# A planned instruction order made anew, and the last 64 rows of a weight prepared on 128 partitions

## The chip, the cores and the metric

The kernel runs on one core of one Trainium2 chip. The metric is the device time of one execution in microseconds (us); the times shown are medians of several runs. The core has five engines with an instruction queue each: TensorE (PE in the profile) multiplies matrices, VectorE (DVE), ScalarE (ACT) and GpSimd (POOL) work on elements, and SyncE (SP) issues most of the transfers. An engine takes its instructions strictly in the order in which they were written, and one that waits holds up all behind it on that engine.

## The reference, cut to what matters

```python
w = softmax(weight_gen, axis=-1)          # (8, 4224, 8 heads, 7 taps)
x_unf = 7 shifted copies of x             # x: (8, 4224, 192), zero-padded in front
y  = einsum('bshk,bskhg->bshg', w, x_unf) # a convolution with weights of its own at each token
xn = (y - mean(y)) / sqrt(var(y) + 1e-6) * g_ln
out = y + relu(xn @ w_ch1) @ w_ch2        # 192 -> 768 -> 192
```

## The kernel before, in words

**Tiling.** The 33,792 tokens lie on 128 partitions, 264 in a row on each. A "column" is one such token position, so one column is 128 tokens. The columns are worked off in parts (`PARTS`, L21: six of 4, six of 8, fifteen of 12, then 8 and 4), and within a part in chunks of 4 or 6 columns. The softmax has its own, larger pieces (`SOFT`, L22: 4, 8, then 12 at a time). The feed-forward part works on groups of 4 columns (512 tokens), 66 in all.

**The front half, per chunk.** SyncE loads x into a ring of 36 columns (L311) and the tap weights (L317). The softmax goes VectorE maximum (L340), GpSimd subtraction (L342), ScalarE exponential (L345), VectorE sum (L347) and so on; its result `wn` lies in PSUM. The convolution (`conv`, L370) is three products of two taps each into buffers called `pr` and one product of one tap into `y`, all on VectorE (L404). For taps 1 and 3, GpSimd issues a transfer that adds the second half of the `pr` buffer onto the first (L410, "add" below). GpSimd then adds four pieces onto `y` (L407): the two halves of tap pair 5 first, then the two results of the transfers. A chunk of 4 columns has 768 elements in each partition.

**The norm and the turn.** ScalarE takes sums (L448) and squares (L453) of `y`, one row of statistics follows on ScalarE and VectorE (L476 to L487), ScalarE scales (L499, `xh`) and writes a half-precision high part (L515, `hl`), GpSimd writes the low part (L517, also into `hl`), and SyncE issues a transposing transfer (L521, "turn") that makes `xT`, the layout that TensorE needs.

**The back half, per group.** TensorE multiplies `xT` with the first weight (L531). One group is three units; a unit is 16 wide matmuls, and eight narrow ones finish a unit and begin the next, so two units share them. A unit fills one of two `ph` buffers in PSUM. ScalarE evicts it with relu (L561, `hh`), VectorE evicts what half precision lost (L563, `hlo`), and then the `ph` buffer is free for the unit after the next. The second weight needs 4 outputs of 18 matmuls each per group (L600 to L602, `po`), VectorE adds them to `y` (L613), and SyncE stores `y` (L620).

**The weights.** They come as 64-bit words and are turned into 32-bit numbers by `from_double` (L652: one ScalarE square, four VectorE steps, one ScalarE square with a sum), scaled by a power of two (`w_scale`, L687) and split into a high and a low half-precision part (L741 to L761). The first weight has 192 rows: 128 of them lie on 128 partitions (`a`), and the last 64 on the first 64 partitions alone (`c`). Transfers (`shift`, L748) copy half-precision rows to the other 64 partitions, where the layout of `xT` wants them. The second weight (`c2`) is turned in three pieces, and its low part is made by GpSimd at L780.

**What sets the order.** Nothing is written straight away. Each step becomes an `Op` (L66) with an engine, an estimated cost and a due time `want`, which is the column where it is used less a lead from a table (`WANT`, L30, `W_WANT` for the weights, `FIRST` for a correction in the first 12 columns). `Plan.order` (L92) then plays the program through once: at each step it takes, for each engine, the ready step with the smallest due time among those that could start within `AHEAD` ns of the earliest, and places the earliest of these, provided that its due time is within `WINDOW` columns of the oldest unplaced step. The written order follows from the planned start times. Adds and turns are kept apart: a turn waits until the add planned before it has landed, and an add for the turn (L117, L153 to L156, L812).

Of the kernel before, what the change touches and what calls it, by code (L numbers as in the profile page):

```python
# [9 lines left out]
F32 = mybir.dt.float32  # L10
# [6 lines left out]
P = 128  # L17
# [31 lines left out]
class Op:  # L49
    __slots__ = ("rank", "eng", "cost", "want", "fn", "lat", "dma", "deps", "nxt", "left", "ready",  # L50
                 "bufs", "start", "end", "kind", "behind")


class Plan:


    DMA_START = {"SP": 900.0, "Pool": 650.0, "ACT": 1250.0}
# [8 lines left out]
    def op(self, eng, cost, want, fn, r=(), w=(), lat=120.0, dma=0.0, kind=None):  # L66
# [3 lines left out]
        o.rank, o.eng, o.cost, o.want, o.fn, o.lat, o.dma = len(self.ops), eng, cost, want, fn, lat, dma  # L70
# [21 lines left out]
    def order(self):  # L92
        tenant = {p: [None] * len(t) for p, t in self.pools.items()}
        free, cand, dma_free, out = {}, {}, 0.0, []

        last, clear = {"add": None, "turn": None}, {"add": 0.0, "turn": 0.0}
        for o in self.ops:
            o.left = len(o.deps)
            for d in o.deps:
                d.nxt.append(o)  # L100
            cand.setdefault(o.eng, [])
            free[o.eng] = 0.0
            if not o.left:
                cand[o.eng].append(o)
# [21 lines left out]

        by_want, lead = sorted(self.ops, key=lambda o: o.want), 0
        while len(out) < len(self.ops):
# [24 lines left out]
            if o.kind:  # L153
# [14 lines left out]
def kernel(  # L168
# [72 lines left out]
    def dma_ns(n):  # L241
        return n * P / 370.0
# [45 lines left out]
    def sp(want, fn, r, w, dma, kind=None):  # L288
        op("SP", 1400 if kind else 450, want, fn, r=r, w=w, dma=dma, kind=kind)

    def load_x(ch):
        t0, n = ch["S"], ch["n"]
        want = t0 - WANT["load"]
        if t0 == 0:

            def first():
# [5 lines left out]
            sp(want, first, [], [("x", "h"), *cols], dma_ns((PAD + n) * D))  # L302
            src = bass.AP(tensor=xf.tensor, offset=0, ap=[[PB * C * D, B], [1, n * D]])
            sp(want, lambda: SY.dma_start(X[0:B, PAD : PAD + n, :].rearrange("p t d -> p (t d)"), src), [],
               [("x", "f")], 300.0)
            return
        if t0 % RING == 0:
            op("ACT", 1050, t0 - WANT["conv"] - 3,
# [3 lines left out]
           [xkey(t) for t in range(t0, t0 + n)], dma_ns(n * D * 4))  # L312

    def load_w(pa):
        t0, n = pa["S"], pa["n"]
        wb = pa["w"] = Buf("w")
        sp(t0 - WANT["wload"], lambda: SY.dma_start(at(wb)[:, :n, :].rearrange("p t f -> p (t f)"), tokens(wf, t0, n)), [], [wb],  # L317
           dma_ns(n * HK * 4))

    def early(s, what):  # L320
        return s - FIRST[what] * max(0.0, 1 - s / 12)

    def softmax(pa):
        n, S0, wb = pa["n"], early(pa["S"], "soft"), pa["w"]
# [11 lines left out]
        def step(eng, cost, name, fn, r, w):  # L336
            op(eng, cost, S0 - WANT[name], fn, r, w)
# [23 lines left out]
        step("V", 2 * v_ns(m, 20), "inv", newton, ["sm", rr], ["sm"])  # L361
# [482 lines left out]
```

## Time and profile before

| | us |
|---|---|
| median of 3 runs | 907.81 (907.77 to 909.34) |
| the profiled execution, as timed | 908.86 |
| its span in the profile | 907.1 |
| TensorE busy | 815.0 |
| VectorE busy | 785.3 |
| GpSimd busy | 696.6 |
| ScalarE busy | 676.5 |

The granted clock of TensorE was 0.992 of the full one over the span. The profile's views give times from the span's start. In a row of the timeline the first number is the start, the second the duration, then come engine, line, operation, output and input; in brackets stands how long the engine had been idle before and what released it. A row with x2 merges two instructions. Idle time of an engine that nobody waits for costs nothing.

### The profile page before, as it was taken

The numbers are of one execution on the slowest core, as the hardware profiler recorded it, in microseconds if no ns is written. First come the engines' busy times: TensorE is split into PE (matmuls) and PEld (weight loads), VectorE is DVE, ScalarE is ACT, GpSimd is POOL, SyncE is SP. The second block draws the span as 40 slices with busy tenths as digits, with TensorE's granted clock in tenths as the row PEclk, the third lists the DMA queues.
The fourth block names the chain that finished last, engine by engine and source line by source line (L and its number), as shares of the span: only waits on it lengthen the run. The fifth ranks groups of instructions, "written<-read, shape, count | busy, mean of one in ns | idle before, by whom it ended". The sixth has DMA issues, their size and how long they took to land. (4 is left out here: it accounts for less than half of the span.)

```text
span 907.1 us, 21485 instructions
## 1 busy us (share of the span) xinstructions
PE 815.0 (90%) x8716; PEld 729.6 (80%) x8716; DVE 785.3 (87%) x833; ACT 676.5 (75%) x1773; POOL 696.6 (77%) x403
## 2 busy tenths in 40 slices
PE   0035999999999999999999999999999999999997
PEld 0023898789888989898888898888988898799997
DVE  6897999999998989899798899988989979884342
ACT  2577878888878976986876896888698688599321
POOL 2799999998988788889877879878886986894000
PEclk9996999999999999999999999999999999999999
DMA  8867787798888777779776879867787666656111
GB/s 218 218 139 157 150 189 159 163 192 190 174 167 186 181 160 173 153 163 198 158 172 150 181 173 177 170 152 173 172 180 156 141 132 149 129 114 107 47 52 54
DMA packets 137996, 142.23 MB, mean 157 GB/s; under 512 B 107496, under 2 KB 108904, under 8 KB 137896
## 3 DMA queue, kind: packets, MB, share of 16 engines
q1 hardware_dynamic: 122983, 88.95, 42.3%
q0 software_dynamic: 14688, 51.91, 30.0%
q8 instruction: 68, 1.11, 0.5%
q14 instruction: 33, 0.26, 0.1%
q10 hardware_dynamic: 224, 0.00, 0.0%
HBM read 36.43 MB, written 25.95 MB: 69 GB/s over the span
## 5 line engine op out<-in xcount | busy, mean ns | idle before, releaser
L407 POOL TENSOR_TENSOR y<-y,pr 128x1152 f32<-128x1152 f32 (+1 forms) x204 | 506.0, 2516 | 71.4 <-DVE pr L404 66.4
L600 PE MATMUL po<-c_w2h,hh 128*128 128x192 f16 x1584 | 390.4, 246 | 0.0
L602 PE MATMUL po<-c_w2h,hlo 128*128 128x192 f16 x1584 | 390.0, 246 | 0.0
L601 PE MATMUL po<-c_w2l,hh 128*128 128x192 f16 x1584 | 390.0, 246 | 0.0
L531 PE MATMUL ph<-xT,c_w1h 128*128 128x256 f16 x2376 | 328.8, 275 | 26.0 <-DVE hlo L563 19.3
L404 DVE TENSOR_TENSOR pr<-x,wn 128x2304 f32<-128x2304 f32 (+1 forms) x153 | 337.3, 2216 | 9.7 <-POOL y L407 3.6
L563 DVE SCALAR_TENSOR_TENSOR hlo<-ph,hh 128x1024 f16<-128x1024 f32 x198 | 238.2, 1217 | 72.1 <-ACT hh L561 71.9
L531 PEld LDWEIGHTS <-c_w1h 128*128 128x128 f16 x2376 | 227.3, 99 | 69.9 <-issue 45.0
L561 ACT ACTIVATE hh<-ph 128x1024 f16<-128x1024 f32 x198 | 200.2, 1012 | 89.4 <-PE ph L531 86.6
L531 PE MATMUL ph<-xT,c_w1l 128*128 128x256 f16 (+1 forms) x1584 | 210.2, 274 | 7.3 <-DMA xT<-hl 5.8
L600 PEld LDWEIGHTS <-hh 128*128 128x128 f16 x1584 | 155.1, 98 | 7.6 <-issue 6.3
L601 PEld LDWEIGHTS <-hh 128*128 128x128 f16 x1584 | 155.2, 98 | 1.4 <-issue 0.2
L602 PEld LDWEIGHTS <-hlo 128*128 128x128 f16 x1584 | 155.1, 98 | 0.2 <-DVE hlo L563 0.2
L499 ACT ACTIVATE xh<-y,s 128x192 f32<-128x192 f32 x264 | 123.7, 535 | 31.8 <-DVE s L487 29.3
L531 PEld LDWEIGHTS <-c_w1l 128*128 128x128 f16 (+1 forms) x1584 | 108.8, 97 | 39.3 <-issue 21.3
L517 POOL TENSOR_TENSOR hl<-xh,hl 128x768 f16<-128x768 f32 x66 | 117.1, 1809 | 26.2 <-ACT hl L515 24.3
L410 POOL DMA_DIRECT2D pr<-pr x102 | 100.6, 1043 | 33.9 <-DVE pr L404 25.4
L453 ACT ACTIVATE junk<-y,s 128x192 f32<-128x192 f32 x264 | 119.4, 452 | 6.7
L448 ACT ACTIVATE junk<-y 128x192 f32<-128x192 f32 x264 | 95.1, 360 | 25.8 <-POOL y L407 20.0
L613 DVE SCALAR_TENSOR_TENSOR y<-po,c_fs,y 128x384 f32<-128x384 f32 x132 | 77.6, 608 | 17.3 <-PE po L602 17.3
L404 DVE TENSOR_TENSOR y<-x,wn 128x1152 f32<-128x1152 f32 (+1 forms) x51 | 60.0, 1179 | 0.0
L515 ACT ACTIVATE hl<-xh 128x768 f16<-128x768 f32 x66 | 55.0, 833 | 0.3
(62 smaller groups left out, 328.2 us busy)
## 6 DMA issues: line engine op xcount, KB each, us to landing
pr<-pr POOLq DMA_DIRECT2D x60, 576.0 KB, 6.1
x<-in_x_dram SPq DMA_DIRECT2D x30, 576.0 KB, 5.4
out_dram<-y SPq DMA_DIRECT2D x30, 576.0 KB, 4.5
pr<-pr POOLq DMA_DIRECT2D x42, 384.0 KB, 6.5
out_dram<-y SPq DMA_DIRECT2D x21, 384.0 KB, 4.0
x<-in_x_dram SPq DMA_DIRECT2D x20, 384.0 KB, 7.2
w<-in_weight_gen_dram SPq DMA_DIRECT2D x21, 336.0 KB, 6.1
pr<-in_moe_w_ch_dram SPq DMA_DIRECT2D x1, 1152.0 KB, 16.9
```

The lines of the kernel that those rows point to most:

```text
L404: V.tensor_tensor(out=ov, in0=xv, in1=wv, op=ALU.mult)
L407: E.tensor_tensor(out=flat(0), in0=flat(0), in1=flat(k), op=ALU.add)
L410: return Q.dma_start(flat(to), flat(k), accum_op=ALU.add, max_dma_last_dim=CHUNK * D * 4)
L453: A.activation(junk, at(y)[:, j, :], AF.Square, bias=at(s4)[:, 3, t : t + 1], accum_out=at(s4)[:, 0, t : t + 1])
L499: A.activation(at(xh)[:, t, :], at(y)[:, i, :], AF.Identity, bias=at(s4)[:, 3, g + t : g + t + 1], scale=at(s4)[:, 1, g + t : g + t + 1])
L517: lambda xh=xh, hl=hl: Q.tensor_tensor(out=halves(hl, True), in0=pairs(xh), in1=halves(hl, False), op=ALU.subtract),
L531: T_.matmul(at(gp["ph"][u])[:, r, v * 2 * P : (v + 1) * 2 * P], W[w][rows, wb, (2 * u + v) * P : (2 * u + v + 1) * P], xv[rows, r, xb, :, ...
L561: lambda: A.activation(at(hh)[:, us, :], at(ph), AF.Relu), [ph], [(hh, u)])
L563: lambda: V.scalar_tensor_tensor(out=at(hlo)[:, us, :], in0=at(ph), scalar=0.0, in1=at(hh)[:, us, :], op0=ALU.max, op1=ALU.subtract),
L600: T_.matmul(o, tok(hh, j), w2h[:, j, :], start=(j == 0), stop=False)
L601: T_.matmul(o, tok(hh, j), w2l[:, j, :], start=False, stop=False)
L602: T_.matmul(o, tok(hlo, j), w2h[:, j, :], start=False, stop=(j == NF - 1))
```

## The change

The diff leaves the computation and its tiling (`PARTS`, `SOFT`, all buffers) as they are, and changes four things.

1. **The table of leads.** `WANT` has two numbers for each kind of step: a lead, and what is added to it at column 0, falling to nothing at column 3.7 (`RAMP`). `W_WANT` and `FIRST` go; the weights' steps have entries in the same table, and more kinds have one of their own. `AHEAD` is 0. A step's due time is lowered to that of the earliest step that needs it.
2. **The planner's costs.** Each queue of transfers has its own free time in place of one for all, with 250 bytes per ns in place of 370; an issue costs 620 ns, in place of 450; a matmul block has a latency of 420, 80 or 360 ns, other steps 140.
3. **Loads.** They carry the kind "load" and are held to a window of their own (`NEAR`, 29.84 columns).
4. **The weight's last 64 rows.** Each row of 768 numbers is loaded as two halves on two partitions, so `from_double("c", ...)` and the scaling work on 128 partitions x 384. The high and low halves are made in a spare part of the tile `hh`, and eight transfers of 64 partitions x 384 put them in place, where before two of 64 x 768 did; the gain `g` of these rows is loaded twice.

```diff
-WANT = {'load': 38.96, 'wload': 44.01, 'max': 25.94, 'sub': 29.98, 'exp': 32.11, 'sum': 24.37,
...
-AHEAD = 55.78
-WINDOW = 20.72
+WANT = {'load': (-3.03, -19.38), 'wload': (75.89, -46.46), 'max': (34.08, -74.96), 'sub':
...
+RAMP = 3.7
+AHEAD = 0.0
+WINDOW = 20.41
+NEAR = 29.84
...
+        lead, more = WANT[want[0]]
+        s = want[1]
+        o.want = s - lead - more * max(0.0, 1 - s / RAMP)
...
+        for o in reversed(self.ops):
+            for d in o.deps:
+                d.want = min(d.want, o.want)
...
-            until = by_want[lead].want + WINDOW
+            until, near = by_want[lead].want + WINDOW, by_want[lead].want + NEAR
...
-                rows = [(t, o) for t, o in ((earliest(o), o) for o in c if o.want <= until)
+                rows = [(t, o) for t, o in ((earliest(o), o) for o in c
+                                          if o.want <= (near if o.kind == "load" else until))
...
-                dma_free = max(t + o.cost + self.DMA_START[o.eng], dma_free) + o.dma
-                o.end = dma_free + self.DMA_END
-            if o.kind:
+
+                begin = max(t + o.cost + self.DMA_START[o.kind if o.kind == "turn" else o.eng],
+                            dma_free.get(o.eng, 0.0))
+                dma_free[o.eng] = begin + o.dma * (1.0 if o.kind == "turn" else 1.2)
+                o.end = dma_free[o.eng] + self.DMA_END
+            if o.kind in clear:
...
-        dma("SP", SY, "load", lambda: words(1, 0, 2 * F)[top, :], w1b[P:D, :], 4 * F, raw[1])
+        dma("SP", SY, "load", lambda: words(1, 0, F),
+            bass.AP(tensor=w1b.tensor, offset=P * 2 * F, ap=[[F, 2], [2 * F, 64], [1, F]]), 4 * F, raw[1])
...
-        from_double("c", lambda: words(1, 0, 2 * F)[top], lambda: f32(wc, F)[top], F, s1[top, 1:2],
-                    [raw[1]], [wc], rows=top)
+        from_double("c", lambda: words(1, 0, F), lambda: f32(wc, F2), F2, s1[:, 1:2], [raw[1]], [wc])
...
+        def halves(w, tmp, r, name):
+            for i, rows in enumerate((top, bot)):
+                fs = slice(i * F2, (i + 1) * F2)
+                shift(w[top, 1, fs], lambda rows=rows: tmp()[rows], r, [(name + "1t", i)], F2)
+                shift(w[bot, 2, fs], lambda rows=rows: tmp()[rows], r, [(name + "2b", i)], F2)
```

Three places show how the order moves. The names in the rows: `pr` are product buffers, `y_67` to `y_71` the chunks 0 to 4, `hl_83` and `hl_84` the half-precision parts of groups 0 and 1, `xT_85` and `xT_86` what the turns of these groups write, `hh_88` and `hh_89` the raw rows of the first weight, `ph_103` and `ph_104` scratch for it. Lines above 310 are shifted by 15 to 30 in the changed kernel.

VectorE before, behind the first three products of chunk 0 and a sum of the softmax: the weight's steps, and at the end the third product of two taps of chunk 0, into `pr_78`.

```order
L672 TENSOR_SCALAR ph_103<-hh_89 64x768
L672 TENSOR_SCALAR ph_104<-hh_88 128x768
L675 SCALAR_TENSOR_TENSOR ph_103<-hh_89,ph_103 64x768
L675 SCALAR_TENSOR_TENSOR ph_104<-hh_88,ph_104 128x768
L678 SCALAR_TENSOR_TENSOR ph_103<-hh_89,ph_103 64x768
L678 SCALAR_TENSOR_TENSOR ph_104<-hh_88,ph_104 128x768
L357 SCALAR_TENSOR_TENSOR wn_102<-wn_102,rr_95 128x64
L358 SCALAR_TENSOR_TENSOR wn_102<-wn_102,rr_95 128x64
L682 SCALAR_TENSOR_TENSOR hlo_90<-pr_78,ph_104 128x768
L682 SCALAR_TENSOR_TENSOR hlo_90<-pr_79,ph_103 64x768
L340 TENSOR_REDUCE mx_92<-w_66 128x96
L404 TENSOR_TENSOR pr_78<-x,wn_102 128x2x768
```

VectorE now, from the first product of chunk 0 on:

```order
L423 TENSOR_TENSOR pr_76<-x,wn_102 128x2x768
L423 TENSOR_TENSOR pr_77<-x,wn_102 128x2x768
L361 TENSOR_REDUCE mx_93<-w_65 128x64
L423 TENSOR_TENSOR y_67<-x,wn_102 128x768
L423 TENSOR_TENSOR pr_79<-x,wn_102 128x2x768
L368 TENSOR_REDUCE wn_102<-e_97 128x64
L689 TENSOR_SCALAR ph_103<-hh_88 128x768
L361 TENSOR_REDUCE mx_92<-w_66 128x96
L692 SCALAR_TENSOR_TENSOR ph_103<-hh_88,ph_103 128x768
L689 TENSOR_SCALAR ph_104<-hh_89 128x384
```

The third product of chunk 0 (now into `pr_79`) moved ahead of all steps of the weight, behind one maximum and the product into `y_67`; the weight's rows with 64 partitions x 768 are rows with 384 elements now.

GpSimd before, from the low part of group 0 on to some rows behind that of group 1 (DMA rows are adds):

```order
L517 TENSOR_TENSOR hl_83<-xh_81,hl_83 128x2x384
L407 TENSOR_TENSOR y_69<-y_69,pr_80 128x768
L407 TENSOR_TENSOR y_69<-y_69,pr_78 128x768
L407 TENSOR_TENSOR y_69<-y_69,pr_79 128x768
L410 DMA pr_77<-pr_77 128x768
L410 DMA pr_76<-pr_76 128x768
L407 TENSOR_TENSOR y_70<-y_70,pr_80 128x768
L517 TENSOR_TENSOR hl_84<-xh_82,hl_84 128x2x384
L410 DMA pr_78<-pr_78 128x768
L407 TENSOR_TENSOR y_70<-y_70,pr_80 128x768
L410 DMA pr_79<-pr_79 128x768
```

GpSimd now, from the last row of chunk 1 on to the same place:

```order
L426 TENSOR_TENSOR y_68<-y_68,pr_76 128x768
L429 DMA pr_77<-pr_77 128x768
L429 DMA pr_80<-pr_80 128x768
L426 TENSOR_TENSOR y_69<-y_69,pr_78 128x768 x2
L429 DMA pr_76<-pr_76 128x768
L426 TENSOR_TENSOR y_69<-y_69,pr_77 128x768
L429 DMA pr_78<-pr_78 128x768
L426 TENSOR_TENSOR y_69<-y_69,pr_80 128x768
L532 TENSOR_TENSOR hl_84<-xh_82,hl_84 128x2x384
L426 TENSOR_TENSOR y_70<-y_70,pr_79 128x768 x2
L426 TENSOR_TENSOR y_70<-y_70,pr_76 128x768
```

Before, the low part of group 1 (`hl_84`) stood between the pieces of chunk 3 and had two adds close behind it; now it stands behind the last piece of chunk 2, its nearest add is two rows ahead of it, and the next one comes only behind three further pieces.

SyncE before, from the loads ahead of the weight's shifts to the turn of group 1:

```order
L311 DMA x<-in_x_dram 128x1x768 x3
L642 DMA pr_80<-in_moe_w_ch_dram 128x6x384
L317 DMA w_65<-in_weight_gen_dram 128x1x672
L311 DMA x<-in_x_dram 128x1x768
L748 DMA c_w1h<-c_w1h 64x768 x3
L748 DMA c_w1l<-c_w1l 64x768 x3
L317 DMA w_66<-in_weight_gen_dram 128x1x672
L311 DMA x<-in_x_dram 128x1x768
L521 DMA_TRANSPOSE xT_85<-hl_83 128x12x128
L311 DMA x<-in_x_dram 128x1x768 x2
L521 DMA_TRANSPOSE xT_86<-hl_84 128x12x128
```

SyncE now:

```order
L341 DMA w_66<-in_weight_gen_dram 128x1x672
L341 DMA w_64<-in_weight_gen_dram 128x1x672
L770 DMA c_w1h<-c_w1h 64x768 x2
L770 DMA c_w1h<-hh_89 64x384 x4
L770 DMA c_w1l<-c_w1l 64x768 x2
L770 DMA c_w1l<-hh_89 64x384 x4
L536 DMA_TRANSPOSE xT_85<-hl_83 128x12x128
L335 DMA x<-in_x_dram 128x1x768 x3
L536 DMA_TRANSPOSE xT_86<-hl_84 128x12x128
```

Six shifts (L748) became twelve (L770), and one load of x stands among these rows and the first turn no more; seven chunks of x are issued ahead of the first turn now, ten before.

More of the change, by code (lines that the diff above doesn't have):

```diff
@@ L50 @@
     __slots__ = ("rank", "eng", "cost", "want", "fn", "lat", "dma", "deps", "nxt", "left", "ready",
-                 "bufs", "start", "end", "kind", "behind")
+                 "bufs", "start", "end", "kind", "behind", "key")
 class Plan:
-    DMA_START = {"SP": 900.0, "Pool": 650.0, "ACT": 1250.0}
+    DMA_START = {"SP": 900.0, "Pool": 900.0, "ACT": 1250.0, "turn": -950.0}
     DMA_END = 1000.0
@@ L311, in load_x @@
         sp(want, lambda: SY.dma_start(X[:, xcol(t0) : xcol(t0) + n, :].rearrange("p t d -> p (t d)"), tokens(x, t0, n)), [],
-           [xkey(t) for t in range(t0, t0 + n)], dma_ns(n * D * 4))
+           [xkey(t) for t in range(t0, t0 + n)], dma_ns(n * D * 4), "load")
     def load_w(pa):
@@ L316, in load_w @@
         wb = pa["w"] = Buf("w")
[L317 to L321, printed above, removed]
+        sp(("wload", t0), lambda: SY.dma_start(at(wb)[:, :n, :].rearrange("p t f -> p (t f)"), tokens(wf, t0, n)), [], [wb],
+           dma_ns(n * HK * 4), "load")
     def softmax(pa):
-        n, S0, wb = pa["n"], early(pa["S"], "soft"), pa["w"]
+        n, S0, wb = pa["n"], pa["S"], pa["w"]
         m = n * H
@@ L547, in narrow_products @@
                        stop=(first and v == 1))
[L549 removed]
+    W1S = ["h0", "l0", "h1b", "l1b", "l2t", "h2t"] + [(k, i) for k in ("h1t", "l1t", "h2b", "l2b") for i in range(2)]
     def at_unit(unit):
@@ L559, in evict @@
         su = at_unit(unit)
-        op("ACT", a_ns(2 * NT * P, 50), su - WANT["relu"],
+        op("ACT", a_ns(2 * NT * P, 50), ("relu", su),
            lambda: A.activation(at(hh)[:, us, :], at(ph), AF.Relu), [ph], [(hh, u)])
-        op("V", v_ns(2 * NT * P, 6), su - WANT["hlo"],
+        op("V", v_ns(2 * NT * P, 6), ("hlo", su),
            lambda: V.scalar_tensor_tensor(
@@ L602, in mm @@
                 T_.matmul(o, tok(hlo, j), w2h[:, j, :], start=False, stop=(j == NF - 1))
-        op("PE", 1494, s, mm, [*((hh, u) for u in range(3)), *((hlo, u) for u in range(3)), "w2"],
-           [(po, h)])
+        op("PE", 1490, (f"o{t}", s), mm, [*((hh, u) for u in range(3)), *((hlo, u) for u in range(3)), "w2"],
+           [(po, h)], lat=360.0)
         if h == 0:
@@ L666, in tv @@
             return a[rows].bitcast(dt)[:, :n]
-        want = -W_WANT[want]
-        op("ACT", a_ns(n), want, lambda: A.activation(mv(), part(1).bitcast(F32), AF.Square), r, [m])
+        squared, want, normed = ((f"w_{want}{p}", 0) for p in "svn")
+        op("ACT", a_ns(n), squared, lambda: A.activation(mv(), part(1).bitcast(F32), AF.Square), r, [m])
         op("V", v_ns(n), want,
@@ L763, in weights @@
+        shift(w1l[bot, 1, :], lambda: w1l[top, 0, :], ["l0"], ["l1b"])
+        shift(w1l[top, 2, :], lambda: w1l[bot, 0, :], ["l0"], ["l2t"])
+        copy("w_h", lambda: f32(wc, F2), lambda: f32(wc, F2), F2, ["gi"], [wc], gi[:, 1:2])
+        low(lc, lambda: f32(wc, F2), hc, F2, [wc, (raw[1], "h")], [(raw[1], "l")])
+        halves(w1l, lc, [(raw[1], "l")], "l")
         tn = NF // 3 * D
```

149 lines of the change are left out of this document (74 added, 75 removed), and 3 rows, old and new, of the table WANT.

## The prediction

> **What bounds the kernel now.** I read the page first, then TensorE's waits, then the windows, then the timeline of the first 95 us.
>
> ```profile
> span 907.1 us, 21485 instructions
> PE 815.0 (90%) x8716; PEld 729.6 (80%) x8716; DVE 785.3 (87%) x833; ACT 676.5 (75%) x1773; POOL 696.6 (77%) x403
> ```
>
> TensorE is busy for 815.0 of 907.1 us, so 92.1 us are idle. Its waits say where they lie, over the span and (last row, asked for the window from 120 us on) in the long stretch:
>
> ```profile
> PE po L692 <- DVE c_s L732: 28.1, 1, 28.1
> PE po L692 <- DVE c_s L768: 25.5, 1, 25.5
> PE ph L531 <- DVE hlo L563: 20.8, 18, 2.6
> PE ph L531 <- DMA xT<-hl: 11.9, 2, 6.2
> ...
> PE ph L531 <- DVE hlo L563: 14.6, 15, 1.8
> ```
>
> The two waits at L692 are the start, before there is anything to multiply. What follows them is 11.9 us for two turns, and 20.8 us for `hlo`, the eviction that frees a `ph` buffer. 14.6 us of the latter, 15 waits with a mean of 0.97 us, lie behind 120 us; no other wait of TensorE is there. How fast TensorE can go when nobody holds it up stands in the chain of waits near the end, and what follows its last matmul too:
>
> ```profile
> 822.99 4.14 PE ph L531 x40
> ...
> 871.60 4.14 PE ph L531 x40
> ...
> 901.89 0.62 DVE y L613
> ```
>
> The pattern stands twice between these two rows, so it takes (871.60 - 822.99) / 2 = 24.3 us; it holds 120 matmuls at L531, six units with their narrow ones, that is two groups: 12.15 us a group, 802 us for all 66. So the span is a start, 802 us, what TensorE loses on the way, and a last eviction and store (907.1 - 901.9 = 5.2 us). The first matmuls show the start and the first loss (TensorE's timeline):
>
> ```profile
> 60.91 1.44 PE L531 MATMUL ph<-xT,c_w1h 128*128 128x256 f16 x6 [6.20 <-DMA xT<-hl]
> ...
> 77.96 0.61 PE L531 MATMUL ph<-xT,c_w1l 64*128 64x256 f16 x4 [5.75 <-DMA xT<-hl]
> 78.50 1.46 PE L531 MATMUL ph<-xT,c_w1h 128*128 128x256 f16 x6
> ...
> 90.98 0.83 PE L531 MATMUL ph<-xT,c_w1h 128*128 128x256 f16 x6
> ```
>
> 60.9 + 802 + 5.2 is 868.1, so 39.0 us of the span are lost on the way: 14.6 behind 120 us, and most of the rest ahead of 100 us, where TensorE waits for the second turn and runs at half pace (six products take 1.46 us at 78.5, 0.83 at 90.98). The windows agree:
>
> ```profile
> 60.00:80.00 20.00, 10.84 (x72) 7.06 (x72) 17.66 (x26) 17.54 (x46) 18.82 (x14) 0.90 0.73 159
> 80.00:100.00 20.00, 17.37 (x150) 14.18 (x149) 16.06 (x20) 14.46 (x42) 18.18 (x13) 0.76 0.62 127
> ...
> 700.00:800.00 100.00, 97.16 (x1048) 87.53 (x1047) 92.43 (x88) 76.47 (x208) 82.80 (x46) 1.00 0.64 134
> ```
>
> Columns: TensorE, weight loads, VectorE, ScalarE, GpSimd, then clock, DMA share, GB/s. In the ramp VectorE and GpSimd are nearly full and TensorE starves; later TensorE is full, VectorE close behind.
>
> **The change, part by part.** What counts is when the second group's `xT` lands, for until then TensorE has only three units to do in either kernel. The rows ahead of it, from four engines' timelines:
>
> ```profile
> 10.55 3.42 DVE L404 TENSOR_TENSOR pr<-x,wn 128x1536 f32<-128x1536 f32 x2 [3.48 <-DMA x<-in_x_dram]
> ...
> 24.17 1.74 DVE L404 TENSOR_TENSOR pr<-x,wn 128x1536 f32<-128x1536 f32 x1
> ```
> ```profile
> 25.99 3.71 POOL L407 TENSOR_TENSOR y<-y,pr 128x768 f32<-128x768 f32 x2 [0.24 <-DVE pr L404]
> ...
> 31.51 3.99 POOL L407 TENSOR_TENSOR y<-y,pr 128x768 f32<-128x768 f32 x2
> ...
> 55.87 1.63 POOL L517 TENSOR_TENSOR hl<-xh,hl 128x768 f16<-128x768 f32 x1
> ...
> 65.92 2.27 POOL L517 TENSOR_TENSOR hl<-xh,hl 128x768 f16<-128x768 f32 x1
> ...
> 69.86 1.84 POOL L410 DMA_DIRECT2D pr<-pr  x1
> ```
> ```profile
> 36.51 1.76 ACT L742 ACTIVATE c_w1h<-hlo,c_gi 128x768 f16<-128x768 f32 x2 [1.20 <-DVE c_gi L737]
> ...
> 50.49 0.83 ACT L515 ACTIVATE hl<-xh 128x768 f16<-128x768 f32 x1
> ```
> ```profile
> 57.53 1.54 SPq L521 DMA_TRANSPOSE xT<-hl  x1
> ...
> 74.72 1.40 SPq L521 DMA_TRANSPOSE xT<-hl  x1
> ```
>
> and the prices, from the groups kept apart by form (0 to 60 us) and the DMA issues of the same window (the second add row: 60 to 120 us):
>
> ```profile
> L404 DVE TENSOR_TENSOR pr<-x,wn 128x1536 f32<-128x1536 f32 x11 | 19.1, 1747 | 3.5 <-DMA x<-in_x_dram 3.5
> ...
> L672 DVE TENSOR_SCALAR po<-pr 128x384 int32<-128x384 int32 x3 | 1.6, 554 | 2.2 <-DMA pr<-in_moe_w_ch_dram 2.2
> ...
> L672 DVE TENSOR_SCALAR ph<-hh 64x768 int32<-64x768 int32 x1 | 1.0, 953 | 0.5 <-DMA hh<-in_moe_w_ch_dram 0.5
> ```
> ```profile
> L407 POOL TENSOR_TENSOR y<-y,pr 128x768 f32<-128x768 f32 x11 | 21.3, 1940 | 1.3 <-DVE c_s L768 0.8 <-DVE pr L404 0.2
> ...
> L410 POOL DMA_DIRECT2D pr<-pr x6 | 5.6, 941 | 11.5 <-DVE pr L404 11.5
> ...
> L745 POOL TENSOR_TENSOR c_w1l<-hlo,c_w1h 128x768 f16<-128x768 f32 x1 | 1.9, 1940 | 0.0
> ```
> ```profile
> pr<-pr POOLq DMA_DIRECT2D x6, 384.0 KB, 7.0
> ...
> c_w1h<-c_w1h SPq DMA_DIRECT2D x3, 96.0 KB, 2.1
> ```
> ```profile
> pr<-pr POOLq DMA_DIRECT2D x10, 384.0 KB, 4.6
> ```
>
> *Chunk 0 first.* Before, chunk 0's third product stood behind the weight's steps and began at 24.17, so its `y` was complete at 31.51 + 3.99 = 35.5. Now it follows the product into `y`: two products end at 10.55 + 3.42 = 14.0, then a maximum (0.5, in proportion to its 448 elements), half a product (0.9) and the third (1.75), 17.2 (x is also issued one place earlier, which I count at nothing). GpSimd adds two pieces (3.7) to 20.9, one subtraction of 672 elements (1.7 in proportion), and two more pieces (4.0): `y` is complete at 26.6, 8.9 us earlier.
>
> *The weight on 128 partitions.* 64 partitions cost as much as 128 (953 ns for 64 x 768), 384 elements 554: four VectorE steps save 0.4 us each, 1.6; two of ScalarE's copies and GpSimd's low part (1.94 to about 1.0) save as much in proportion. Six more shifts go onto SyncE's queue ahead of the first turn. Three issues in a row take 1.80 us at 37.47 in SyncE's timeline:
>
> ```profile
> 37.47 1.80 SPq L748 DMA_DIRECT2D c_w1h<-c_w1h  x3
> ```
>
> so four cost 2.4 us behind the low part's second half. The cover is GpSimd, which between that half and the low part of group 0 still has one addition (1.94) and the low part itself (1.63): 3.6 us. Cover gone, it would cost up to 2.4. [...]
>
> *The first turn.* GpSimd sets it. On VectorE, from 17.2: the weight's eight steps (4 x 0.95 + 4 x 0.55 = 6.0), some 5 us of softmax and scaling (2,900 elements at the product's rate, and a dozen small ones), three products and a half (6.1): chunk 1's third product ends near 34.5. GpSimd follows: addition 1.94, low parts 1.94 and 1.0, addition 1.94, low part of group 0 1.63: 43.0. ScalarE has the same work as between 36.5 and 51.3 before it (14.8 us, from 26.6 on: 41.4) and is no later. So the turn is issued at 43, not 57.53: 14.5 us earlier, and TensorE starts at 46.4.
>
> *The second turn.* Before, group 1's low part was done at 65.92 + 2.27 = 68.2, but the turn left at 74.72: it was kept apart from the add issued behind the low part, at 69.86. Now the nearest add stands ahead. From 43.0: two additions (3.9), three issues to the second add (0.9 each by its row, 2.7), two (3.9), one, the add of `pr_78`, one, the low part (1.94 + 0.9 + 1.94 + 1.63 = 6.4): 59.9. The add is issued 4.5 us ahead of that, at 55.4 to 56.3, and lands 4.6 to 7.0 us later, at 60 to 63.3. VectorE's third product for it is the eleventh pair: 11 x 1.75, and the rest of the queue, near 55. So the turn leaves at 60 to 64 in place of 74.72, 11 to 14.7 us earlier; 2 less if VectorE's product slips, 2 more if products and additions overlap as tightly as the two products in 3.42 us do. I take 13.5, bounds 9 and 17. Behind this turn SyncE holds loads of x; ten chunks are issued by then, and VectorE is at the fourth, so nobody waits for those.
>
> *The half pace.* TensorE started twice at half pace, at 60.9 and 77.96, and will start twice so again. The Trainium skill ("TensorE: Matmul & The Clock Gate", HAM oscillation) has it that an idle gap above 3.4 us halves the clock until about as long a stretch of work. By it the longer gap now (three units at half pace end near 54; a turn takes 3.4 us to the first matmul, 57.53 to 60.91, so the second ends it near 66) costs no more than before, and the sum stays.
>
> *Behind the ramp.* The tables and costs move hundreds of rows, and no row of the trace prices the new mix. What TensorE must cover is relu and `hlo`:
>
> ```profile
> L563 DVE SCALAR_TENSOR_TENSOR hlo<-ph,hh 128x1024 f16<-128x1024 f32 x198 | 238.2, 1217 | 72.1 <-ACT hh L561 71.9
> ...
> L561 ACT ACTIVATE hh<-ph 128x1024 f16<-128x1024 f32 x198 | 200.2, 1012 | 89.4 <-PE ph L531 86.6
> ```
>
> 2.2 us plus whatever stands ahead of them on their engines. Counted in TensorE's written order, a `ph` buffer finds one output or none between its last use and its next one 47 times of 196 before and 35 times now, three outputs or more 47 times before and 69 now. Bounds: all 14.6 us of `hlo` waits go, or they double. I take a little under half gone, 6.5, since VectorE's long products still stand in the queue ahead of `hlo`. Loads held back cost nothing unless x is late: a load is issued still some 18 columns ahead of the additions, over 50 us at 12.15 us per 4 columns, against landings of about 7.
>
> *Sum.* 908.86 (the profiled execution; 907.1 of span and 1.8 around it) - 13.5 - 6.5 = 888.9; it is 1.05 above the median of the runs, so 887.8, say 888.
>
> **The rivals.**
>
> *The early start is given back (901).* The ramp is bounded by GpSimd and VectorE (18.8 and 17.7 of 20 us busy), so groups may come so slowly that TensorE works in bursts. Each burst starts cold: the window from 80 to 100 lost 17.4 x 0.24 = 4.2 us by its clock of 0.76. Three such restarts in groups 2 to 6 return 12.6 of the 13.5. For it: both engines are full. Against: the front half had run ahead by 120 us without a further wait for a turn. 901 with the later gain.
>
> *VectorE's queue (slower, 928).* `hlo` stands in one queue with the products, and a new mix may put a product right ahead of it more often. Should one in four of the 198 units wait 0.97 us, 48.5 us replace 14.6: 907.8 - 13.5 + 33.9 = 928. It decides from 31 waits on, where gain and loss meet. Against: only 15 of some 185 units waited so far.
>
> *No waits at all (880).* Every `hlo` wait behind the ramp goes: 907.8 - 13.5 - 14.6 = 879.7. For it: TensorE's order has longer covers. Against: VectorE is 92% busy there.
>
> *The order is no better than the old one on the chip (907).* The planner's model differs from the chip, and gains and losses cancel.
>
> **How the numbers follow.** Forecast 0.62 (880 to 896), given back 0.15, no waits 0.11, VectorE's queue 0.08, no better 0.04. The range 876 to 903 holds the forecast, most of the no-waits case and nearly all of the given-back case. Faster by over 0.2% (1.8 us, about what a measurement can tell) is 0.62 + 0.15 + 0.11 = 0.88, the same 0.04, slower 0.08.
>
> **What would show it.** Right: first matmul at L546 near 46, the second turn's idle ending at 63 to 68, and TensorE's `hlo` waits behind 120 us near 8 us. Wrong: a second turn behind 70, several waits for xT behind 80 us, `hlo` waits above 20 us, or VectorE waiting for x.

## The result and the profile after

The changed kernel takes 903.21 us (median of 4 runs, 901.05 to 903.7), the kernel before 908.01 (4 runs): a ratio of 0.994 with a 95% interval of 0.9921 to 0.9959. It is faster by 4.8 us, where 20 were forecast. The profiled executions, 908.86 and 901.05 us, are 7.8 us apart: that of before lies above its median, that of after is the fastest of its four. So the profiles say where time went, and the medians how much. The other three runs of the changed kernel took 902.94 to 903.7 us at a granted clock of 0.985 to 0.986, against 901.05 at 0.991 in the profiled one; what they lost beyond it stands in no trace.

The page of the changed kernel, its first lines:

```profile
span 899.2 us, 21468 instructions
...
PE 813.2 (90%) x8716; PEld 728.8 (81%) x8716; DVE 781.7 (87%) x833; ACT 675.7 (75%) x1773; POOL 694.4 (77%) x403
```

TensorE's waits of the changed kernel, over the span and then from 120 us on (columns: us in total, times, longest):

```profile
PE po L709 <- DVE c_s L749: 33.7, 1, 33.7
PE ph L546 <- DMA xT<-hl: 27.6, 5, 18.8
PE ph L546 <- DVE hlo L578: 16.2, 17, 3.1
...
PE ph L546 <- DVE hlo L578: 13.0, 15, 3.1
PE ph L546 <- DMA xT<-hl: 2.9, 3, 1.6
```

Before, TensorE waited 14.6 us behind 120 us, all for `hlo`. Now it is 13.0 + 2.9 = 15.9. The forecast 6.5 us of gain there is not there at all. The ramp in TensorE's timeline:

```profile
53.02 1.44 PE L546 MATMUL ph<-xT,c_w1h 128*128 128x256 f16 x6 [18.76 <-DMA xT<-hl]
...
70.01 0.61 PE L546 MATMUL ph<-xT,c_w1l 64*128 64x256 f16 x4 [6.03 <-DMA xT<-hl]
```

The first matmul came at 53.0 (60.9 before, 46.4 forecast), and the second turn's wait ended at 70.0 (78.0 before, 63 to 68 forecast). So the second group came 7.95 us earlier, and the span gained as much: 907.1 - 899.2 = 7.9. The start is later than forecast for a reason that one row of VectorE shows, in the middle of the weight's steps. Here are two rows of the changed kernel, then the first step on the same rows of the weight before:

```profile
18.68 0.95 DVE L692 SCALAR_TENSOR_TENSOR ph<-hh,ph 128x768 int32<-128x768 int32 x1
26.75 0.56 DVE L689 TENSOR_SCALAR ph<-hh 128x384 int32<-128x384 int32 x1 [7.12 <-DMA hh<-in_moe_w_ch_dram]
```
```profile
16.11 1.81 DVE L672 TENSOR_SCALAR ph<-hh 64x768 int32<-64x768 int32 x2 [0.54 <-DMA hh<-in_moe_w_ch_dram]
```

In brackets: VectorE was idle for 7.12 us, until the load of the weight's last 64 rows had landed. Before, it had waited 0.54 us there. In the queue of SyncE both loads of the first weight were issued when they were before (4.30 there). The load of the second weight then stood in this queue until the rows had come (it was issued at 17.44 before). The rows below are SyncE's issues, its wait up to 40 us, and the load's time from issue to landing in the kernel before:

```profile
4.34 1.23 SPq L657 DMA_DIRECT2D hh<-in_moe_w_ch_dram  x2
...
26.75 0.40 SPq L657 DMA_DIRECT2D pr<-in_moe_w_ch_dram  x1
```
```profile
SPq L657 <- DMA hh<-in_moe_w_ch_dram: 11.6, 1, 11.6
```
```profile
hh<-in_moe_w_ch_dram SPq DMA_DIRECT2D x1, 384.0 KB, 11.1
```

So the load needed some 21 us (from the end of its issue at 5.57 to 26.75) in place of 11.1. What the DMA engines did from 16 to 27 us, in the changed kernel and then before (40 slices; a digit is the busy share of the 16 engines in tenths):

```profile
DMA  9999999999999999999895431111011111111110
GB/s 279 246 235 223 246 223 201 246 201 223 201 279 257 268 290 257 290 268 279 223 246 134 89 78 34 22 45 45 22 45 56 56 45 56 56 45 56 50 59 39
```
```profile
DMA  9989979899899999999979997999989999999999
```

From about 22.6 us on the engines are busy to a tenth and move some 50 GB/s, in a stretch in which the kernel before had sevens to nines and 190 to 420 GB/s. Taken in windows of 1 us and less, the share is 0.12 to 0.14 from 23 to 26.7 us: about two of 16 engines. The source of the new load is written with two halves of a row as its slowest dimension, `[[F, 2], [2 * F, 64], [1, F]]`. That gave the first theory.

### The profile page after: what moved, and what is told of

The parts are those of the page before. It is cut to its first block, busy times and chain, and to the rows that moved or that the text cites. A ratio compares the mean times of both kernels' runs of the same rounds, so it can differ in the third digit from the quotient of the medians.

```text
span 899.2 us, 21468 instructions
## 1 busy us (share of the span) xinstructions
PE 813.2 (90%) x8716; PEld 728.8 (81%) x8716; DVE 781.7 (87%) x833; ACT 675.7 (75%) x1773; POOL 694.4 (77%) x403
## 4 chain that ended last, share of the span: by engine, by line
PE 26%; DVE 12%; POOL 9%; ACT 8%; DMA 6%; issue 5%; SPq 0%; POOLq 0%; DVEq 0%
PE ph L546 13%; POOL y L426 7%; DVE pr L423 7%; PE po L615 5%; PE po L617 4%; PE po L616 4%; DMA xT<-hl 3%; DVE hlo L578 3%; ACT hh L576 3%; ACT junk L468 2%; DMA pr<-pr 2%; ACT junk L463 1%; DVE y L423 1%; POOL hl L532 1%; DVE y L628 1%
## 5 line engine op out<-in xcount | busy, mean ns | idle before, releaser
L532 POOL TENSOR_TENSOR hl<-xh,hl 128x768 f16<-128x768 f32 x66 | 118.8, 1868 | 15.9 <-ACT hl L530 15.8
L429 POOL DMA_DIRECT2D pr<-pr x102 | 96.2, 1003 | 34.5 <-DVE pr L423 20.9
L628 DVE SCALAR_TENSOR_TENSOR y<-po,c_fs,y 128x384 f32<-128x384 f32 x132 | 79.8, 608 | 28.2 <-PE po L617 28.1
```

Of the source, the lines that this page charges most:

```text
L532: lambda xh=xh, hl=hl: Q.tensor_tensor(out=halves(hl, True), in0=pairs(xh), in1=halves(hl, False), op=ALU.subtract),
```

## The experiments

Theory A: a load whose source has a slowest dimension of 2 is moved by 2 DMA engines; this late load holds up the ramp. Rival B: the ramp's gain is given back in any case, since GpSimd and VectorE are full. All ratios are to the kernel before.

**Two loads.** The changed kernel with the same bytes in the same places, but as two transfers of 64 partitions.

```diff
-        dma("SP", SY, "load", lambda: words(1, 0, F),
-            bass.AP(tensor=w1b.tensor, offset=P * 2 * F, ap=[[F, 2], [2 * F, 64], [1, F]]), 4 * F, raw[1])
+        def cut():
+            for i, rows in enumerate((top, bot)):
+                d = SY.dma_start(words(1, 0, F)[rows, :], w1b[P:D, i * F : (i + 1) * F])
+            return d
...
```

> The changed kernel with one edit: the last 64 rows of W1 are loaded by two transfers of 64 partitions each in place of one whose source has an outermost dimension of 2. Same bytes, same place, same order of all else. Theory A (the new load ran on 2 of the 16 DMA engines and VectorE waited 7.1 us for it): that wait falls below 1 us, the second turn's matmuls start near 63 in place of 70.0, and the time falls by 6 to 8 us against the changed kernel, to 894 to 897 us. Theory B (the ramp gives an earlier start back, since VectorE and GpSimd are full): the wait falls as well, but the time stays within 2 us of 903.

896.88 us (895.43 to 898.99), ratio 0.9879 (0.9859 to 0.9898): 6.3 us less than the changed kernel (5.6 by the spans of the two profiles), 10.8 less than the kernel before in the same session. VectorE's wait for the rows is gone. VectorE's first step on them, the DMA issues, SyncE's two turns and TensorE's ramp of this kernel:

```profile
18.95 0.55 DVE L693 TENSOR_SCALAR ph<-hh 128x384 int32<-128x384 int32 x1
```
```profile
hh<-in_moe_w_ch_dram SPq DMA_DIRECT2D x2, 192.0 KB, 8.3
```
```profile
42.80 1.54 SPq L536 DMA_TRANSPOSE xT<-hl  x1
...
59.83 1.42 SPq L536 DMA_TRANSPOSE xT<-hl  x1
```
```profile
46.16 1.44 PE L546 MATMUL ph<-xT,c_w1h 128*128 128x256 f16 x6 [18.82 <-DMA xT<-hl]
...
63.06 0.61 PE L546 MATMUL ph<-xT,c_w1l 64*128 64x256 f16 x4 [6.16 <-DMA xT<-hl]
```

With the rows on time, the ramp runs as it was forecast: first turn at 42.8 (43 forecast), first matmul at 46.2 (46.4), second turn at 59.8 (60 to 64), its wait over at 63.1 (63 to 68). The second turn is no longer held by an add, as GpSimd's rows show (L429 issues an add, L532 is the low part of group 1):

```profile
55.49 0.88 POOL L429 DMA_DIRECT2D pr<-pr  x1
...
57.87 1.94 POOL L532 TENSOR_TENSOR hl<-xh,hl 128x768 f16<-128x768 f32 x1
...
65.29 0.86 POOL L429 DMA_DIRECT2D pr<-pr  x1
```

The low part was done at 57.87 + 1.94 = 59.81, and the turn left at 59.83. The span is 893.6 us: of 14.9 us in the ramp, 13.5 reach the end of the profiled execution, which is the fastest of its five; by the medians 10.8 do. B falls: the late load held up the ramp. That its slowest dimension made it late is not shown by this run, since two transfers of 64 partitions differ from one of 128 in more than that.

**The kernel before, its load cut in two.** Its load with a source of two blocks of 32 rows.

```diff
-        dma("SP", SY, "load", lambda: words(1, 0, 2 * F)[top, :], w1b[P:D, :], 4 * F, raw[1])
+        dma("SP", SY, "load", lambda: words(1, 0, 2 * F)[top, :],
+            bass.AP(tensor=w1b.tensor, offset=P * 2 * F, ap=[[64 * F, 2], [2 * F, 32], [1, 2 * F]]), 4 * F, raw[1])
```

> The kernel before with one edit: the source of the load of W1's last 64 rows is written as 2 x 32 rows in place of 64; same bytes, same partitions, same order. Theory A (an outermost dimension of 2 puts the load on 2 of 16 engines): the load lands near 26 us in place of 16, VectorE waits 7 to 10 us at the first step on it, and the time rises by 6 to 9 us, to 914 to 917. Rival (what made the new load late is the half rows or what else was queued then, not the outermost dimension): the load lands by 18 us and the time stays within 2 us of 908.

908.0 us (906.86 to 909.81), ratio 0.9999 (0.9986 to 1.0012), where A expected 914 to 917. The load landed 11.7 us behind its issue, as it had (11.1). Taken alone, this speaks against A. But the second block begins where the first one ends, so the two dimensions describe one run of 64 rows: the edit may have changed nothing. It settles nothing, and the next one was made for it.

**The same with a slowest dimension that can't be merged.** Even rows first, then odd ones, so the second block begins inside the first. The rows lie on their partitions in another order, so the weight's rows are permuted; the work is the same. The last line is a second run with 8, a value between 2 and the 64 of the kernel before.

```diff
-            bass.AP(tensor=w1b.tensor, offset=P * 2 * F, ap=[[64 * F, 2], [2 * F, 32], [1, 2 * F]]), 4 * F, raw[1])
+            bass.AP(tensor=w1b.tensor, offset=P * 2 * F, ap=[[2 * F, 2], [4 * F, 32], [1, 2 * F]]), 4 * F, raw[1])
...
+            bass.AP(tensor=w1b.tensor, offset=P * 2 * F, ap=[[2 * F, 8], [16 * F, 8], [1, 2 * F]]), 4 * F, raw[1])
```

> The kernel before, with one edit: the last 64 rows of the first weight are read with a source whose slowest dimension is 2 (even rows, then odd ones; 32 each), so they lie on their 64 partitions in another order, which changes the products and not the work. In the earlier try the two dimensions of the source lay behind one another without a gap and made one. Theory A (the slowest dimension of the source sets how many of the 16 DMA engines move a load): DMA engines are down to 2 of 16 until the load lands, more than 20 us behind its issue in place of some 12, VectorE waits 5 to 10 us for it, and the time grows by 4 to 9 us over 908. Rival B (the load was slow in the changed kernel because of its 128 partitions of half a row each, or because other loads stood in its way): landing and time as before, 908.

> The kernel before, with the same load from a source whose slowest dimension is 8, the next one 8 (rows in another order on their partitions). Theory A: 8 of 16 DMA engines, so the load itself takes twice as long as over 16 and a quarter as long as over 2; it lands 2 to 5 us later than before and well ahead of the one with 2; the time is within 3 us of 908. Rival B: landing as before.

With 2: 919.23 us (918.38 to 919.98), ratio 1.0131 (1.0116 to 1.0146). With 8: 909.05 us (906.38 to 910.33), ratio 1.0008 (0.9993 to 1.0023). VectorE's first step on these rows, and the DMA engines from 20 to 31 us, with 2:

```profile
30.66 1.81 DVE L673 TENSOR_SCALAR ph<-hh 64x768 int32<-64x768 int32 x2 [15.71 <-DMA hh<-in_moe_w_ch_dram]
```
```profile
DMA  9999998999998999999799967421111101110111
```

and VectorE's step with 8:

```profile
17.25 1.81 DVE L673 TENSOR_SCALAR ph<-hh 64x768 int32<-64x768 int32 x2 [2.22 <-DMA hh<-in_moe_w_ch_dram]
```

The wait is 0.54 us with the rows in one piece, 2.22 with 8 and 15.71 with 2, and with 2 the busy share falls to a tenth again until the rows land. Only the pattern in which the source is read differs between these kernels, so A is shown for 2, on a kernel that has nothing else of the change. The price, 10.9 us, was above the 4 to 9 us expected, as the wait was above the 5 to 10: of the 11.6 us by which the second group came later, 10.7 reached the end of the span. With 8 the effect is small: the step began at 17.25, 1.1 us later than before, where 2 to 5 were expected, and only 0.6 later than with the two blocks of 32 rows (16.67). So the runs show the case of 2, and no clear scale from 2 upwards.

The Trainium skill has this rule in "DMA: Bandwidth & Descriptors" (Why a DMA increments its semaphore by 16 and not by 1): the number of engines is the largest one up to 16 that divides the slowest dimension of both sides. By it the load on 128 partitions from a source with 2 outermost gets 2 engines, and the one with 8 gets 8. The busy share of 0.12 to 0.14 in the changed kernel (2 of 16 is 0.125) agrees for 2; no slice isolates the load with 8.

**The order with the old weight.** The changed kernel without its fourth part (the last 64 rows on 64 partitions again; the main lines of the edit).

```diff
-        from_double("c", lambda: words(1, 0, F), lambda: f32(wc, F2), F2, s1[:, 1:2], [raw[1]], [wc])
+        from_double("c", lambda: words(1, 0, 2 * F)[top], lambda: f32(wc, F)[top], F, s1[top, 1:2],
+                    [raw[1]], [wc], rows=top)
```

> The changed kernel without its fourth part: W1's last 64 rows stay on 64 partitions, loaded, scaled and shifted as before; tables, planner and costs are the new ones, the planner orders the few other weight steps itself. Theory A: the load is on time, so the time is 1 to 2 us above that of the run with two loads, 895 to 899. Theory B: within 2 us of 903.

904.18 us (902.78 to 904.79), ratio 0.9956 (0.9939 to 0.9972), span 901.9. That is outside of the 895 to 899 that A gave, and it meets the number of B, though not for B's reason. The first matmul is in time, the second group is not:

```profile
46.51 1.44 PE L546 MATMUL ph<-xT,c_w1h 128*128 128x256 f16 x6 [18.34 <-DMA xT<-hl]
62.63 0.58 PE L707 MATMUL po<-c_s,ones 128*128 128x1 f32 x2 [7.73 <-DVE c_s L784]
76.03 0.61 PE L546 MATMUL ph<-xT,c_w1l 64*128 64x256 f16 x4 [12.28 <-DMA xT<-hl]
```

What held the second group stands in GpSimd's and SyncE's rows:

```profile
62.74 1.75 POOL L532 TENSOR_TENSOR hl<-xh,hl 128x768 f16<-128x768 f32 x1
...
66.26 0.87 POOL L429 DMA_DIRECT2D pr<-pr  x1
...
68.62 1.20 POOL L429 DMA_DIRECT2D pr<-pr  x1
```
```profile
72.80 4.19 SPq L536 DMA_TRANSPOSE xT<-hl  x2
```

The low part of group 1 was done at 64.5, but two adds stand behind it ahead of the turn, which left at 72.80, 8.3 us later; SyncE's waits put this down to an add. It is the hold of the kernel before (68.2 to 74.72), back in an order that was derived for other steps.

**The old order with the new weight.** The kernel before with the fourth part alone, its rows in two loads (edit as above, from one to the other).

> The kernel before with the fourth part alone, its load made by two transfers: W1's last 64 rows on 128 partitions under the old tables and planner. Theory A: the weight's steps are 1.6 us shorter on VectorE and the first turn 0 to 2 us earlier, but the second turn waits for an add as before, so the time is 906 to 908. A fall by more than 3 us would mean that the weight's steps, not the order, set the second turn.

916.67 us (914.1 to 920.68), ratio 1.0097 (1.0074 to 1.012): slower, where 906 to 908 were expected, though it does less work on VectorE. Its second group came at 76.12, held by an add again (low part done at 66.1, turn at 72.89). Then TensorE waited 4.06 us for `hlo` at 84.31 and 5.97 us at 93.86 for the low part of the second weight, which GpSimd began at 91.30, 9.7 us later than in the kernel before. The order is derived again for each set of steps, so neither of these two runs prices a part by itself: in both, a table did worse with steps that it was not made for.

**Where the gain behind the ramp went.** Idle time of TensorE, summed over the rows of its timeline that show 0.15 us or more (us; the last column is what the span holds behind the second group's first matmul):

| kernel | second group | 120 to 220 | 220 to 405 | 405 on | span | rest |
|---|---|---|---|---|---|---|
| before | 77.96 | 3.3 | 3.8 | 7.5 | 907.1 | 829.1 |
| after | 70.01 | 6.2 | 6.9 | 2.7 | 899.2 | 829.2 |
| two loads | 63.06 | 6.5 | 6.9 | 1.9 | 893.6 | 830.5 |
| before, load with 2 | 89.51 | 4.4 | 3.8 | 7.4 | 917.8 | 828.3 |
| new order, old weight | 76.03 | 3.3 | 4.4 | 2.3 | 901.9 | 825.9 |
| old order, new weight | 76.12 | 1.0 | 1.7 | 11.3 | 915.3 | 839.2 |

The new order does save waits from 405 us on (7.5 to 1.9), but it has about as many more between 120 and 405. Hence the nearly constant rest of some 829 us in the first four rows: where only the load differs, most of the second group's shift goes to the end (10.7 of 11.6 us, and 5.6 of 7.0). The last two rows, with orders of their own, do not follow that. Nor do the medians quite: with a median's span (1.8 us less than its time) and the second group of the profile, an estimate, the rest is 828 us before and with the load of 2, but 831 and 832 in the changed kernel and with two loads. So in most runs the new order has some 3 to 4 us more behind the second group than the old one, if their ramps are those of the profiles. With two loads GpSimd is full while the groups come (columns: TensorE, weight loads, VectorE, ScalarE, GpSimd):

```profile
60.00:80.00 20.00, 12.35 (x97) 9.45 (x97) 18.66 (x29) 18.17 (x47) 19.84 (x14) 0.77 0.50 109
80.00:100.00 20.00, 19.99 (x218) 18.12 (x216) 19.77 (x25) 18.45 (x53) 20.00 (x14) 1.00 0.81 185
100.00:120.00 20.00, 19.68 (x219) 17.71 (x216) 18.67 (x23) 13.65 (x41) 19.20 (x13) 1.00 0.69 151
120.00:200.00 80.00, 73.83 (x775) 65.47 (x776) 74.96 (x87) 65.05 (x173) 71.25 (x49) 0.98 0.78 175
```

Theory A of the next two runs: GpSimd makes `y` late, and through ScalarE and VectorE `hlo`. Rival B: VectorE's own queue. Both kernels are the one with two loads, with less work for one engine in the columns below 72 and the same written order. The first leaves out GpSimd's addition of tap 6 there; the second makes tap 5 alone on VectorE and adds it twice (a line that shortens the output of this product is left out below).

```diff
-            op("Pool", q_ns(nd), (f"a{i}", t0), lambda k=k, h=h: add(k + h),
+            op("Pool", q_ns(nd), (f"a{i}", t0), lambda k=k, h=h: None if h and t0 < 72 else add(k + h),
```
```diff
-            op("V", v_ns(2 * nd if k else nd), (f"c{i}", t0), lambda k=k: mul(k, 2 if k else 1),
+            op("V", v_ns(2 * nd if k else nd), (f"c{i}", t0), lambda k=k: mul(k, 2 if k and not (k == 5 and t0 < 72) else 1),
...
-            op("Pool", q_ns(nd), (f"a{i}", t0), lambda k=k, h=h: add(k + h),
+            op("Pool", q_ns(nd), (f"a{i}", t0), lambda k=k, h=h: add(k if h and t0 < 72 else k + h),
```

> The kernel of the two loads, but in the chunks below column 72 (18 chunks) GpSimd leaves out one of its four additions, that of the second half of tap pair 5, so y lacks tap 6 there; the written order of all other steps is the same. 18 times 1.9 us of additions go from GpSimd, nearly all between 20 and 260 us. Theory A (behind the ramp GpSimd was made the bound: it is full to 124 us in the kernel of the two loads, so y, and with it hlo, comes late): TensorE's idle time from 60 to 400 us falls by 5 us or more, the time by 5 to 10 us below the kernel of the two loads (896.9). Rival B (VectorE's full queue makes hlo late, GpSimd is off the path): idle time behind 120 us is as with two loads, 13 to 15 us, and the time is within 2 us of 896.9.

> The kernel of the two loads, but in the chunks below column 72 (18 chunks) VectorE's third product makes tap 5 alone (768 elements in place of 1,536), and GpSimd adds this piece twice, so its load is the same and y has tap 5 twice and no tap 6 there; the written order is the same. 18 times 0.85 us of products go from VectorE. Theory A (GpSimd is the bound from 40 to 124 us): the first waits, up to 130 us, stay (xT 1.5 and hlo 3.5 us at 121 and 127), and the time falls by less than 2 us below 896.9. Rival B (VectorE's queue): hlo waits from 120 to 400 us fall to less than half of their 9 us, and the time by 4 us or more.

Less for GpSimd: 892.05 us (890.21 to 892.25), ratio 0.9823 (0.9807 to 0.9839), 4.8 us below the two loads. Less for VectorE: 895.55 (893.7 to 896.66), ratio 0.9868 (0.9851 to 0.9885), whose interval overlaps that of the two loads. ScalarE's wait for GpSimd's `y`, with two loads and then with the relief of GpSimd:

```profile
116.73 0.36 ACT L463 ACTIVATE junk<-y 128x192 f32<-128x192 f32 x1 [3.98 <-POOL y L426]
```
```profile
113.47 0.36 ACT L463 ACTIVATE junk<-y 128x192 f32<-128x192 f32 x1 [0.40 <-POOL y L426]
...
120.00:200.00 80.00, 76.70 (x827) 68.77 (x822) 77.45 (x90) 66.28 (x174) 59.38 (x42) 1.00 0.76 169
```

TensorE's idle time fell by 0.5 us from 60 to 120 and by 2.3 (6.5 to 4.2) from 120 to 220; between 220 and 405 it went from 6.9 to 6.3. So GpSimd is a bound behind the ramp, up to about 200 us. It is worth less than the 5 to 10 us expected: 4.8 us by the medians and 3.4 by the spans, for 18 additions of some 1.9 us. The idle time fell by 3.5 us up to 405, where A expected 5 or more up to 400, and behind 120 us it is 13.1, which B allowed too; the time, outside of B's 2 us, and the wait for `y` speak for A. With VectorE relieved, the wait for `hlo` at 127 us stayed at 3.4, as A had it, and the one of 1.5 for xT at 121, which should have stayed too, was gone.

**The waits between 220 and 405 us.** The same two edits for columns 72 to 143 (`72 <= t0 < 144` in the place of `t0 < 72`): first VectorE relieved, by tap 5 twice and no tap 6, then GpSimd, by tap 6 left out.

> The kernel of the two loads, but in columns 72 to 143 (12 chunks of 6 columns) VectorE's third product makes tap 5 alone (1,152 elements in place of 2,304, some 1.25 us less each, 15 us in all), and GpSimd adds this piece twice: y has tap 5 twice and no tap 6 there. The written order is the same, and the products of these columns run from about 200 to 400 us, the stretch in which TensorE waits 6.9 us for hlo between 220 and 400 us with two loads. Theory V (in that stretch VectorE, 97% busy from 200 to 300 us, makes hlo late): these 6.9 us fall below 3.5, and the time by 3 to 5 us below 896.9. Rival G (GpSimd makes it late): they stay between 6 and 8, the time within 1.5 us of 896.9. Rival O (the order itself, with hlo or relu written late, makes the waits, whatever the engines' load): neither this run nor the next one halves them.

> The kernel of the two loads, but in columns 72 to 143 (12 chunks of 6 columns) GpSimd leaves out its addition of tap 6 (some 2.6 us each, 31 us in all), so y lacks tap 6 there; the written order is the same. Theory V (VectorE makes hlo late between 220 and 400 us): the 6.9 us of waits there stay between 6 and 8, the time within 1.5 us of 896.9. Rival G (GpSimd does): they fall below 3.5, the time by 3 to 5 us. Rival O (the order itself): they stay, as with VectorE relieved.

VectorE relieved: 894.66 us (890.72 to 896.9), ratio 0.985 (0.9822 to 0.9877), idle 6.5 us in that stretch, though VectorE's busy time from 300 to 400 us fell from 91.75 to 83.94. GpSimd relieved: 897.56 us (894.24 to 898.0), ratio 0.9878 (0.9858 to 0.9898), idle 7.7. Neither run halves the 6.9 us, and both intervals overlap that of the two loads: what is left of the three is rival O, the written order, by exclusion. Two of these waits, with two loads (1.8 of the 6.9 us), show how it acts. At 303 us, TensorE's last matmuls of a unit, ScalarE's rows up to its relu, VectorE's eviction and TensorE's next unit:

```profile
297.56 0.93 PE L546 MATMUL ph<-xT,c_w1l 128*128 128x256 f16 x10
```
```profile
300.82 0.34 ACT L372 ACTIVATE rr<-wn,bias 128x96 f32<-128x96 f32 x1 [2.74 <-DVE pr L423]
301.19 0.28 ACT L373 ACTIVATE rr<-rr 128x96 f32<-128x96 f32 x1
301.38 1.00 ACT L576 ACTIVATE hh<-ph 128x1024 f16<-128x1024 f32 x1
```
```profile
302.42 1.23 DVE L578 SCALAR_TENSOR_TENSOR hlo<-ph,hh 128x1024 f16<-128x1024 f32 x1 [1.63 <-ACT hh L576]
```
```profile
303.70 0.81 PE L546 MATMUL ph<-xT,c_w1h 128*128 128x256 f16 x6 [0.39 <-DVE hlo L578]
```

The unit was done at 298.5, but its relu stood behind a step of the softmax that idled 2.74 us for VectorE. At 330 us relu is done by 327.5, and `hlo` stands behind a product of 2.56 us:

```profile
326.49 1.00 ACT L576 ACTIVATE hh<-ph 128x1024 f16<-128x1024 f32 x1
```
```profile
326.72 2.56 DVE L423 TENSOR_TENSOR pr<-x,wn 128x2304 f32<-128x2304 f32 x1
329.19 1.22 DVE L578 SCALAR_TENSOR_TENSOR hlo<-ph,hh 128x1024 f16<-128x1024 f32 x1
```
```profile
330.46 0.71 PE L546 MATMUL ph<-xT,c_w1h 128*128 128x256 f16 x5 [1.39 <-DVE hlo L578]
```

That the order makes them fits with another thing: the kernel before and the one with the load of 2, 11 us apart, have the same waits in the same places of their order (0.37, 0.69, 0.71, 0.18 and 1.83 us behind 245 us, with the first at 249.1 and at 259.9). With VectorE relieved the wait at 330 shrinks to 0.20, and new ones of 0.38 and 0.81 follow at 333 and 338. Another order was not tried, so how much of the 6.9 us one could save is open.

The kernel with two loads is faster than both kernels of the case and leaves nothing out; it is the version to keep.

## Why the prediction was wrong

The direction was right (faster, 0.88); the size was not, and 903.2 lies just outside of the range of 876 to 903. Two terms of the sum failed, the ramp by 5.55 us (7.95 for 13.5) and the stretch behind it by 7.8 (a loss of 1.3 for a gain of 6.5). By its steps:

- **"Chunk 0 first" and "The first turn": the first step that failed.** The working counted the weight's eight steps from 17.2 on as if their rows lay ready, as they did before (16.1). They were ready at 26.75. The changed line itself, a source with 2 as its slowest dimension, was in the diff and got no price: the prediction took the transfer's bytes and partitions, and not its shape. This cost some 6 us (903.21 against 896.88 with two loads; 5.6 by the spans), and with it went the first turn (49.67 for 43) and the second (66.75 for 60 to 64).
- **"The second turn", 13.5 us.** Right as a mechanism: turn 2 left without a wait for an add, at 59.83 with two loads, right behind its low part (done at 59.81; 59.9 worked out), and with the old weight, where adds stand behind the low part again, the hold came back. With two loads the gain is 14.9 us in the ramp, inside the bounds of 9 to 17; as made it is 7.95, below them, by the step above.
- **"Behind the ramp", 6.5 us: the second step that failed, in size and in its reason.** The count of outputs that cover `hlo` in TensorE's order said nothing of how late relu and `hlo` themselves start. Measured: 14.6 us of waits before, 15.9 after, 15.3 with two loads. Savings from 405 us on (5.6 us with two loads) are offset by waits ahead of it: up to some 200 us GpSimd makes them in part (relieving it took 2.3 of 6.5 us away), and up to 405 two of them were seen to come from relu and `hlo` written behind a softmax step and a product. The rest of these waits is not explained.
- **"The weight on 128 partitions".** The cover of the shifts held: with two loads the first turn leaves at 42.80, 0.6 us behind the low part of group 0 (40.56 + 1.64 = 42.2) and right behind the last issue of a shift (40.32 + 2.38 = 42.7). So 0.6 of the 2.4 us came through.
- **"The half pace".** It did not cost more: 12.35 x 0.23 = 2.8 us with two loads in the window from 60 to 80, against 10.84 x 0.10 + 17.37 x 0.24 = 5.3 before. This holds for the profiled executions; the other runs of the changed kernel had a granted clock of 0.985 to 0.986 over the span, where its profiled one had 0.991.
- **The rivals.** "Given back" gave 901, close to the result, but for another reason: the changed kernel had no cold restarts behind the ramp in its profile (clock 0.99 from 80 to 100 us, 1.00 later), and what the ramp did gain stayed there. That it came so near to 903 is luck: a late load, which it did not have, took most of the difference. It named GpSimd rightly as full. "VectorE's queue" fell: 13.0 us of `hlo` waits behind 120 us, and not 48.5. (Its gain and loss meet at 29 waits, (13.5 + 14.6) / 0.97, and not at 31.) "No waits at all" fell with the same 13.0 us, and "no better" by 4.8 us that are clear of the interval.

By its own sum with the two measured terms: 908.86 - 7.95 + 1.3 = 902.2 for the profiled execution, which took 901.05. With the load in two transfers the result would have been 896.9, inside the range: so the first step decided that the range was missed, and the second kept the gain at 10.8 us of 20 even then.

## What to carry to other kernels

When a change rewrites the access pattern of a transfer, price the pattern, not only its bytes: read the slowest dimension of the source, and look in the DMA view for a stretch in which the busy share falls to a few engines. A cut of rows into halves went well here as two transfers; one transfer with the rows outermost was not tried. And look at the engine that fed the ramp before promising a second gain from "longer covers": here GpSimd was full from 60 to 120 us, and relieving it was worth some 5 us.

## What the runs showed of the hardware

- The same 384 KB landed 11.1 us behind their issue with 64 rows outermost, and some 21 and 25 us behind it with 2 (the changed kernel, and the one before with the load of 2). Towards the end of the load, at a busy share of 0.12 to 0.14 of 16 engines, 49 to 55 GB/s moved from 24 to 26.7 us: by an estimate some 25 GB/s for each of two engines.
- Two dimensions that lie behind one another without a gap cost nothing here: with 2 blocks of 32 rows the load landed in 11.7 us, against 11.1 with 64 rows.
- A late transfer held up more than its reader: SyncE's queue stood for 11.6 us in the changed kernel, and for 15.3 in the one before with the load of 2, until these rows had landed, ahead of a load into another buffer. What ties the two loads together was not tried.
